# Attention of the later pairs: 128-row chunks with whole scores and one running state, in place of 64-row blocks on quadrants of the array

## The chip, the cores and the metric

The kernel runs on one core of one Trainium2 chip. The metric is the device time of one execution in microseconds. A core has TensorE (PE; its weight loads are shown apart as PEld), VectorE (DVE), ScalarE (ACT), GpSimd (POOL) and SyncE (SP), which run side by side and wait for each other by semaphores. SyncE issues nearly all DMA transfers here.

## The reference, cut to what matters

Retention without a softmax (8 batches, 8 heads, 576 positions, head size 64), and then a mixer of low rank over the positions with a two-layer network:

```
Dmat[h, i, j] = gamma[h] ** (i - j)  if i >= j else 0
x  = ((q @ k.T / 8) * Dmat) @ v                    # heads side by side: 8 x 576 x 512
u  = x + (x.T @ U @ V).T                           # U: 576 x 32, V: 32 x 576
out = u + relu(u @ w_ch1) @ w_ch2                  # 512 -> 2048 -> 512
```

Since gamma ** (i - j) is gamma ** i times gamma ** -j, the kernel scales v by gamma ** -j ahead and the result by gamma ** i behind. What remains of Dmat is a triangular mask, and what lies before a block enters as a state, the running sum of k.T @ v.

## The kernel before, in words

Batches are taken two at a time, as a pair of 2 x 576 = 9 x 128 rows: chunks 0 to 3 are of the even batch, 5 to 8 of the odd one, and chunk 4 (J) holds the last 64 rows of the one and the first 64 of the other. Pair 0 is computed by functions of its own in the start-up and the first stretch (lines 603 to 1009), which the change doesn't touch. Pairs 1 to 3, 27 chunks, go the way that is described here.

**A chunk's way.** `load` (229) fetches k, q and v, three DMAs on SyncE's queue. `prep` (586) casts them: k to bf16 on VectorE in three pieces, because one head of each pair of heads has its two half chunks exchanged between the partition halves (272), q on ScalarE (273), v times its scale on GpSimd in three pieces (281). Then `xbar` (288) transposes q and k with one DMA from SyncE's queue into qkT.

**Attention in sections.** `section(pr, i, n)` (396) works on two chunks at once: scores and states of chunk n, output of chunk i = n - 1. All its matmuls are 64x64 blocks on the four quadrants of TensorE, 64 in a full section: `SC` (305) the two diagonal blocks of the scores of each head, `ST` (367) the sums k.T @ v into AB, one for each half of a chunk, `RV` (325) masked scores times v, `QS` (337) query times state. Scores and output share one PSUM tile, pp, of which there is one. VectorE follows: `mask` (313), the states of the two halves as sums of AB and of an fp32 copy, Af, which ScalarE makes (385 to 394), xt (353), which frees pp for the next section, and two copies of queries to the other half of the partitions (347).

**The mixer.** `MA` (440) forms x.T @ U, `MH` (467) brings it back to the positions, VectorE adds x and gives u (473), and a transposing DMA on SyncE's queue turns u into uT (484), which the next batch's network reads. The odd batch has two such steps, of three and of two chunks.

**The network.** Y1 (523) multiplies uT by w_ch1 and ScalarE applies relu (528); Y2 (557) multiplies by w_ch2, VectorE adds u (546), and GpSimd's queue stores (549).

**What sets the order.** Nothing is scheduled for itself: instructions stand on each engine in the order in which Python issues them, and every queue is worked through in order. `merge` (16) interleaves. Its main list is the network of batch b, with nominal costs: an item of Y1 is 864 or 1080 ns, one of Y2 864, the list 27.6 us for an even batch and 34.6 us for an odd one. The fill list, attention and mixer of batch b + 1, is spread evenly over the first 0.82 of that cost: nine items before the change. The aux list, loads and preps two chunks ahead of a load, is spread over 0.64. The first such stretch has lists and leads of its own (1022 to 1031).

Of the kernel before, what the change touches and what calls it, by code (L numbers as in the profile page):

```python
# [9 lines left out]
FP32 = mybir.dt.float32  # L10
BF16 = mybir.dt.bfloat16
AF = mybir.ActivationFunctionType
# [24 lines left out]
def kernel(  # L37
# [11 lines left out]
    nc = tc.nc  # L49
# [18 lines left out]
    def pool(name, bufs, **kw):  # L68
        return ctx.enter_context(tc.tile_pool(name=name, bufs=bufs, **kw))
# [8 lines left out]
    q2_pool = pool("q2_pool", 2)  # L78
# [15 lines left out]
    triH = consts.tile([P, HALF], BF16, name="triH")  # L94
    Af = consts.tile([P, 2, NHP * D], FP32, name="Af")
# [21 lines left out]
    def early_consts():  # L117
# [32 lines left out]
        nc.vector.tensor_copy(out=triH[0:HALF], in_=tri[0:HALF, 0:HALF])  # L150
        nc.vector.tensor_copy(out=triH[HALF:P], in_=tri[HALF:P, HALF:P])
# [102 lines left out]
    def prep_v(pr, i, rows=slice(0, P)):  # L254
        c = ch[pr, i]
        if "v" not in c:
            c["v"] = v_pool.tile([P, H, D], BF16, tag="v", name="vt")
        scale_rows(c["v"][rows], c["f", 2], i, rows, nc.gpsimd)

    def moves():
        lo, hi = slice(0, HALF), slice(HALF, P)
        return ((slice(0, P), slice(0, P), 0), (lo, hi, 1), (hi, lo, 1))

    def cast_chunk(pr, i):
        c = ch[pr, i]
        c["qk"] = qk_pool.tile([P, 2, dm], BF16, tag="qk", name="qk")
        o = c["qk"][:, 1, :].rearrange("p (hp hl d) -> p hl hp d", hl=2, d=D)
        f = c["f", 1].rearrange("p (hp hl) d -> p hl hp d", hl=2)  # L270
        for to, fr, hl in moves():
            nc.vector.tensor_copy(out=o[to, hl], in_=f[fr, hl])  # L272
        nc.scalar.activation(  # L273
            out=c["qk"][:, 0, :], in_=c["f", 0].rearrange("p h d -> p (h d)"), func=AF.Copy)
        c["v"] = v_pool.tile([P, H, D], BF16, tag="v", name="vt")
        o = c["v"].rearrange("p (hp hl) d -> p hl hp d", hl=2)
        f = c["f", 2].rearrange("p (hp hl) d -> p hl hp d", hl=2)
        w = vscale[:, i, :].rearrange("p (hp hl) -> p hl hp", hl=2)
        for to, fr, hl in moves():
            n = fr.stop - fr.start  # L280
            nc.gpsimd.tensor_tensor(  # L281
                out=o[to, hl], in0=f[fr, hl],
                in1=w[fr, hl, :, None].to_broadcast([n, NHP, D]), op=ALU.mult)

# [9 lines left out]

    def half(n):
        return slice(n * HALF, (n + 1) * HALF)

    def SC(c, pp):  # L300
        qkT = c["qkT"]
        for hp in range(NHP):
            for hl in range(2):
                for m in range(2):
                    nc.tensor.matmul(  # L305
                        pp[half(m), m ^ hl, hp * D:(hp + 1) * D],
                        qkT[half(hl), NHP + hp, half(m)], qkT[half(hl), hp, half(m ^ hl)],
                        start=True, stop=True,
                    )

    def mask(c, pp):
        ret = ret_pool.tile([P, 2, NHP, D], BF16, tag="ret", name="ret")
        nc.vector.tensor_tensor(  # L313
            out=ret.rearrange("p a b i -> p a (b i)").rearrange(
                "p a (b i) -> p a b i", i=D),
            in0=pp[:, :, 0:NHP * D].rearrange("p a (b i) -> p a b i", i=D),
            in1=triH[:, None, None, :].to_broadcast([P, 2, NHP, D]), op=ALU.mult,
        )
        c["ret"] = ret

    def RV(c, pp):
        for hp in range(NHP):
            for hl in range(2):
                for m in range(2):
                    nc.tensor.matmul(  # L325
                        pp[half(m ^ hl), hl, NHP * D + hp * D:NHP * D + (hp + 1) * D],
                        c["ret"][half(m), m ^ hl, hp, :], c["v"][half(m), 2 * hp + hl, :],
                        start=(hp == 0), stop=True, skip_group_check=True,
                    )

    def QS(c, pp, ts):
        for hp in range(NHP):
            for hl in range(2):
                for t in ts:
                    r = half(hl ^ t)
                    qt = c["q2"][r, hp, :] if t else c["qkT"][r, hp, half(t)]
                    nc.tensor.matmul(  # L337
                        pp[half(t), hl, NHP * D + hp * D:NHP * D + (hp + 1) * D],
                        qt, c["S"][r, t, hp, :],
                        start=False, stop=True, skip_group_check=True,  # L340
                    )

    def queries(c):

        c["q2"] = q2_pool.tile([P, NHP, D], BF16, tag="q2", name="q2")
        for x in range(2):
            nc.vector.tensor_copy(  # L347
                out=c["q2"][half(x)], in_=c["qkT"][half(1 - x), 0:NHP, half(1)])

    def XS(pr, i, pp):  # L350
        if ("x", pr) not in st:
            st["x", pr] = x_pool.tile([P, NI, dm], BF16, tag="x", name="xt")
        nc.vector.tensor_tensor(  # L353
            out=st["x", pr][:, i, :].rearrange("p (hp hl d) -> p hl hp d", hl=2, d=D),
            in0=pp[:, :, NHP * D:2 * NHP * D].rearrange("p hl (hp d) -> p hl hp d", d=D),
            in1=qscale[:, i, :].rearrange("p (hp hl) -> p hl hp", hl=2)[
                :, :, :, None].to_broadcast([P, 2, NHP, D]),
            op=ALU.mult,
        )

    def ST(steps):

        for hp in range(NHP):
            for hl in range(2):
                for c, t, start in steps:
                    m, h = t ^ hl, 2 * hp + hl
                    nc.tensor.matmul(  # L367
                        st["AB"][half(hl), t, hp * D:(hp + 1) * D],
                        c["qk"][half(m), 1, h * D:(h + 1) * D], c["v"][half(m), h, :],
                        start=(start and hp == 0), stop=True, skip_group_check=True,  # L370
                    )

    def states(c, i):


        A, Bk = st["AB"][:, 0, 0:NHP * D], st["AB"][:, 1, 0:NHP * D]
        now, old = i % 2, 1 - i % 2
        c["S"] = s_pool.tile([P, 2, NHP, D], BF16, tag="s_sb", name="s_sb")
        S_ = c["S"].rearrange("p s hp d -> p s (hp d)")
        if i == 0:  # L380
            for x in range(2):
                nc.scalar.activation(
                    out=S_[half(x), 1, :], in_=A[half(1 - x)], func=AF.Copy)
        if i != J:
            nc.scalar.activation(out=Af[:, now, :], in_=A, func=AF.Copy)  # L385
        if i == J + 1:
            nc.scalar.activation(out=S_[:, 0, :], in_=Bk, func=AF.Copy)  # L387
        elif i != 0:
            nc.vector.tensor_tensor(out=S_[:, 0, :], in0=Bk, in1=Af[:, old, :], op=ALU.add)
        if i not in (0, J):  # L390
            for x in range(2):
                nc.vector.tensor_tensor(  # L392
                    out=S_[half(x), 1, :], in0=Bk[half(1 - x)],
                    in1=Af[half(1 - x), now, :], op=ALU.add)

    def section(pr, i, n):

        pp = ps_sc.tile([P, 2, 2 * NHP * D], FP32, tag="psc", name="pp")
        if n is not None:
            c = ch[pr, n]  # L400
            SC(c, pp)
            steps = []
            if n in (0, J + 1):
                st["AB"] = ps_o.tile([P, 2, 2 * NHP * D], FP32, tag="po", name="AB")
            if n != J:
                steps.append((c, 0, n in (0, J + 1)))
            if n != 0:
                steps.append((ch[pr, n - 1], 1, n in (1, J + 1)))
            ST(steps)
        if i is not None:  # L410
            RV(ch[pr, i], pp)
            QS(ch[pr, i], pp, {0: (1,), J: (0,)}.get(i, (0, 1)))
        if n is not None:
            mask(c, pp)
            states(c, n)
        if i is not None:
            XS(pr, i, pp)
        if n is not None and n != J:
            queries(c)

    def attn_items(pr, par):
        ks = list(range(0, J + 1) if par == 0 else range(J + 1, NI))
        return [
            lambda i=i, n=n: section(pr, i, n) for i, n in zip([None] + ks, ks + [None])]
# [161 lines left out]
    def prep(g):  # L586
        pr, i = order[g]
        cast_chunk(pr, i)
        xbar(pr, i)
# [421 lines left out]
    with tc.manual_schedule():  # L1011
# [7 lines left out]
        def ready(n):  # L1019
# [10 lines left out]
            starts=(0.3, 0.05, 0.92), leads=(0.81, 0.56, 1.0),  # L1030
# [42 lines left out]
```

## Time and profile before

| | us |
|---|---|
| time, median of 3 runs | 351.9 (349.24 to 354.42) |
| time of the profiled execution | 351.9 |
| its span in the profile | 349.7 |
| TensorE busy | 319.7 (91%) |
| VectorE busy | 174.0 (50%) |
| ScalarE busy | 137.3 (39%) |
| GpSimd busy | 101.5 (29%) |
| mean granted TensorE clock | 0.985 |

Costs per instruction (mean ns of one), of the operations that the change touches:

| line, engine, operation | ns |
|---|---|
| L313 DVE mask, 128x512 | 691 |
| L689 DVE mask of pair 0, 128x1024 | 1222 |
| L389, L392 DVE states, 128x256 and 64x256 | 414, 422 |
| L353 DVE xt, 128x512 | 690 |
| L347 DVE query copies, 64x256 | 261 |
| L272 DVE casts of k, 128x256 and 64x256 | 360, 324 |
| L244 DVE cast of 64x512 | 397 |
| L385 ACT copy of a state sum, 128x256 | 383 |
| L938 ACT copy out of PSUM, 128x512 | 595 |
| L281 POOL scaled v, 128x256 and 64x256 | 623, 612 |
| L248 POOL scaled v, 64x512 | 1041 |
| L473 DVE u, 128x1024, 128x768, 128x512 | 1217, 953, 686 |

A row of the profile's groups names the source line, the engine, what is written from what, and the shape. A wait names who waited, for whom, the sum in us, how often and the longest. Time in a wait costs only where the waiting engine is the bound. Matmuls of TensorE overlap, so their durations don't add; the distance from the start of one group to the start of the next is what a group costs.

### The profile page before, as it was taken

How to read it: one execution, taken by the hardware profiler on the slowest of the kernel's cores; microseconds unless marked ns; L12 is line 12 of the kernel's file. 1: busy time of each engine (PE TensorE's matmuls, PEld its weight loads, DVE VectorE, ACT ScalarE, POOL GpSimd, SP SyncE). 2: the span in 40 equal slices, each digit the busy share in tenths (PEclk: the TensorE clock that was granted, in tenths of full speed). 3: DMA queues.
4: the chain of work that ended last, by engine and by line, in shares of the span. 5: the costliest groups of instructions: out<-in, count | busy, mean ns of one | idle time of the engine just before them, and what ended most of it. 6: DMA issues, size and time to landing. Idle time of an engine off the chain costs nothing.

```text
span 349.7 us, 9092 instructions
## 1 busy us (share of the span) xinstructions
PE 319.7 (91%) x3870; PEld 172.7 (49%) x3870; DVE 174.0 (50%) x358; ACT 137.3 (39%) x298; POOL 101.5 (29%) x169
## 2 busy tenths in 40 slices
PE   8989799999999779979699986988979998999996
PEld 3564445754444334447454443436744454457644
DVE  7654256329743877337554396623955276510021
ACT  3547447871010653047520354107741075017500
POOL 7676760422113622141221314023225120010000
PEclk9999899999999999989989999999999999999999
DMA  7999999984956896937989368996599801240012
GB/s 224 225 212 238 209 206 201 194 154 96 264 150 159 178 210 133 228 80 144 169 160 237 108 125 119 178 221 144 116 174 249 175 32 35 64 128 5 0 62 90
DMA packets 152376, 53.30 MB, mean 152 GB/s; under 512 B 132016, under 2 KB 149808, under 8 KB 152336
## 3 DMA queue, kind: packets, MB, share of 16 engines
q1 hardware_dynamic: 144512, 40.40, 61.1%
q0 software_dynamic: 7824, 12.32, 14.5%
q8 instruction: 30, 0.49, 0.6%
q14 instruction: 10, 0.08, 0.1%
HBM read 36.85 MB, written 9.44 MB: 132 GB/s over the span
## 4 chain that ended last, share of the span: by engine, by line
PE 65%; DMA 19%; DVE 6%; SPq 3%; issue 2%; POOL 2%; ACT 1%; POOLq 0%; DVEq 0%
PE ps_y L557 31%; PE ps_y L523 26%; DMA qkT<-qk 10%; DMA uT<-u 4%; DMA stage_t<-in_q_dram 3%; SPq L617 2%; DMA U_f<-in_moe_U_dram 2%; PE pp L305 2%; DVE s_sb L392 2%; DVE xt L353 1%; PE pp L337 1%; PE ps_y L568 1%; PE ph L467 1%; SPq L229 1%; PE pp L325 1%
## 5 line engine op out<-in xcount | busy, mean ns | idle before, releaser
L528 ACT ACTIVATE y<-ps_y 128x384 bf16<-128x384 f32 (+2 forms) x192 | 90.5, 490 | 135.7 <-PE ps_y L523 135.0
L523 PE MATMUL ps_y<-uT,w_sb 128*128 128x256 bf16 (+2 forms) x768 | 137.4, 333 | 4.8 <-DMA uT<-u 4.6
L557 PE MATMUL ps_y<-w_sb,y 128*128 128x512 bf16 x560 | 126.0, 379 | 0.0
L523 PEld LDWEIGHTS <-w_sb 128*128 128x128 bf16 x768 | 73.0, 99 | 53.7 <-DMA uT<-u 5.6
L557 PEld LDWEIGHTS <-y 128*128 128x128 bf16 x560 | 52.9, 98 | 61.7
L281 POOL TENSOR_TENSOR vt<-stage_t,vscale 64x256 bf16<-64x256 f32 (+1 forms) x81 | 49.9, 616 | 83.2 <-DMA stage_t<-in_v_dram 78.7
L546 DVE TENSOR_TENSOR o_sb<-ps_y,u 128x512 f32<-128x512 f32 (+2 forms) x38 | 25.2, 662 | 81.8 <-PE ps_y L557 79.6
L549 POOL DMA_DIRECT2D out_dram<-o_sb x31 | 17.4, 560 | 114.9 <-DVE o_sb L546 106.0
L313 DVE TENSOR_TENSOR ret<-pp,triH 128x512 bf16<-128x512 f32 x27 | 18.7, 691 | 41.9 <-PE pp L305 21.9
L473 DVE TENSOR_TENSOR u<-ph,xt 128x768 bf16<-128x768 f32 (+2 forms) x24 | 21.8, 952 | 16.8 <-PE ph L467 16.8
L272 DVE CAST qk<-stage_t 64x256 bf16<-64x256 f32 (+1 forms) x81 | 27.2, 336 | 2.6 <-DMA stage_t<-in_k_dram 1.4
L305 PE MATMUL pp<-qkT 64*64 64x64 bf16 x432 | 8.8, 201 | 15.1 <-DMA qkT<-qk 13.8
L353 DVE TENSOR_TENSOR xt<-pp,qscale 128x512 bf16<-128x512 f32 x27 | 18.6, 690 | 4.1 <-PE pp L337 3.6
L305 PEld LDWEIGHTS <-qkT 64*64 64x64 bf16 x432 | 5.9, 110 | 25.5 <-DMA qkT<-qk 18.3
L392 DVE TENSOR_TENSOR s_sb<-AB,Af 64x256 bf16<-64x256 f32 x42 | 17.7, 422 | 1.2 <-ACT s_sb L387 0.7
L273 ACT ACTIVATE qk<-stage_t 128x512 bf16<-128x512 f32 x27 | 16.7, 624 | 2.2 <-DMA stage_t<-in_q_dram 2.2
L385 ACT ACTIVATE Af<-AB 128x256 f32<-128x256 f32 x24 | 9.2, 383 | 16.7 <-PE AB L367 15.8
L689 DVE TENSOR_TENSOR ret<-psc,triU 128x1024 bf16<-128x1024 f32 x8 | 9.6, 1222 | 12.2 <-PE psc L681 12.2
L347 DVE COPY q<-qkT 64x256 bf16<-64x256 bf16 x48 | 12.5, 261 | 1.1
L635 POOL CAST qk<-stage_t 128x512 bf16<-128x512 f32 x16 | 9.7, 616 | 6.4 <-DMA stage_t<-in_v_dram 3.5
L193 PE MATMUL pw<-ident 128*128 128x512 bf16 x31 | 9.8, 461 | 1.4 <-POOL ident masks.py:199 1.4
L446 ACT ACTIVATE a_sb<-pa 128x128 bf16<-128x128 f32 x8 | 2.2, 278 | 21.6 <-PE pa L440 21.6
(112 smaller groups left out, 202.2 us busy)
## 6 DMA issues: line engine op xcount, KB each, us to landing
stage_t<-in_k_dram SPq DMA_DIRECT2D x32, 256.0 KB, 4.7
stage_t<-in_q_dram SPq DMA_DIRECT2D x32, 256.0 KB, 4.8
stage_t<-in_v_dram SPq DMA_DIRECT2D x32, 256.0 KB, 5.7
out_dram<-o_sb POOLq DMA_DIRECT2D x31, 256.0 KB, 3.8
w_sb<-in_moe_w_ch_dram POOLq DMA_DIRECT2D x12, 256.0 KB, 10.1
stage_t<-in_k_dram SPq DMA_DIRECT2D x8, 128.0 KB, 3.4
stage_t<-in_q_dram SPq DMA_DIRECT2D x8, 128.0 KB, 3.4
stage_t<-in_v_dram SPq DMA_DIRECT2D x8, 128.0 KB, 3.4
```

What stands on the lines that cost most here:

```text
L272: nc.vector.tensor_copy(out=o[to, hl], in_=f[fr, hl])
L281: nc.gpsimd.tensor_tensor(out=o[to, hl], in0=f[fr, hl], in1=w[fr, hl, :, None].to_broadcast([n, NHP, D]), op=ALU.mult)
L305: nc.tensor.matmul(pp[half(m), m ^ hl, hp * D:(hp + 1) * D], qkT[half(hl), NHP + hp, half(m)], qkT[half(hl), hp, half(m ^ hl)], start=True ...
L313: nc.vector.tensor_tensor(out=ret.rearrange("p a b i -> p a (b i)").rearrange("p a (b i) -> p a b i", i=D), in0=pp[:, :, 0:NHP * D].rearra ...
L353: nc.vector.tensor_tensor(out=st["x", pr][:, i, :].rearrange("p (hp hl d) -> p hl hp d", hl=2, d=D), in0=pp[:, :, NHP * D:2 * NHP * D].rea ...
L392: nc.vector.tensor_tensor(out=S_[half(x), 1, :], in0=Bk[half(1 - x)], in1=Af[half(1 - x), now, :], op=ALU.add)
L473: nc.vector.tensor_tensor(out=st["u", par][:, i0 - base:i0 - base + n, w].rearrange("p s (c d) -> p c s d", c=2), in0=ph[k][:, :, 0:n, :], ...
L523: nc.tensor.matmul(ps[:, 0:n, :], w1_sb[:, cc, f * P:(f + 1) * P], st["uT", par][:, c0:c0 + n, cc, :], start=(cc == 0), stop=(cc == NCC - 1),)
L528: nc.scalar.activation(out=st["y1", par][:, f, c0 * P:(c0 + n) * P], in_=ps[:, 0:n, :].rearrange("p s t -> p (s t)"), func=AF.Relu)
L546: nc.vector.tensor_tensor(out=o_sb[:, 0:n], in0=ps[:, 0:n], in1=st["u", par][:, c, w], op=ALU.add)
L549: (nc.sync if last else nc.gpsimd).dma_start(out=out_flat[r0:r0 + P, w], in_=o_sb[:, 0:n])
L557: nc.tensor.matmul(ps, st["y1", par][:, f, c * P:(c + 1) * P], w2_sb[:, f, :], start=(f == 0), stop=(f == NF - 1),)
```

## The change

Sections go. A chunk has two items, A and B. A issues the scores of the whole 128x128 block of each head (eight matmuls, 64 rows of the array each), the query by state (eight) into a PSUM tile of its own, po, and the mask of 128x1024 elements. B issues masked scores times v (eight matmuls on the whole array, 64 columns), xt, the state sum of the whole chunk (four matmuls on the whole array), and a ScalarE copy of the running state to bf16. There is one state per batch, kept in PSUM, in place of two sums per chunk. Of chunk J, the mask is block diagonal (triJ), the query by state comes in B and on its first 64 rows alone, and the state sum of its last 64 rows is an item of its own, SJ. The mixed placement of half chunks goes, so k is cast and v is scaled in one instruction each (`cast_qk` and `prep_v`, which pair 0's chunk J uses already), and the copies of queries go. The fill list has 13 items in place of nine. In the first stretch with sections it starts at 0.2 of the cost in place of 0.3.

The diff, cut to its core:

```diff
-    q2_pool = pool("q2_pool", 2)
...
-    triH = consts.tile([P, HALF], BF16, name="triH")
-    Af = consts.tile([P, 2, NHP * D], FP32, name="Af")
+    triJ = consts.tile([P, P], BF16, name="triJ")
...
-        nc.vector.tensor_copy(out=triH[0:HALF], in_=tri[0:HALF, 0:HALF])
-        nc.vector.tensor_copy(out=triH[HALF:P], in_=tri[HALF:P, HALF:P])
+        nc.vector.tensor_copy(out=triJ, in_=tri)
+        nc.vector.memset(triJ[0:HALF, HALF:P], 0.0)
...
-    def moves():
...
-    def cast_chunk(pr, i):
...
-    def SC(c, pp):
+    def SC(pr, i):
+        c = ch[pr, i]
         qkT = c["qkT"]
+        psc = ps_sc.tile([P, 2, NHP, P], FP32, tag="psc", name="psc")
         for hp in range(NHP):
             for hl in range(2):
...
+                r = slice(hl * HALF, (hl + 1) * HALF)
+                nc.tensor.matmul(
+                    psc[:, hl, hp, :], qkT[r, NHP + hp, :], qkT[r, hp, :],
+                    start=True, stop=True,
+                )
+        c["psc"] = psc
...
+    def mask(pr, i):
+        c = ch[pr, i]
+        ret = ret_pool.tile([P, H, P], BF16, tag="ret", name="ret")
+        m = triJ if i == J else tri
         nc.vector.tensor_tensor(
...
+            out=ret.rearrange("p (hp hl) i -> p hl hp i", hl=2), in0=c["psc"],
+            in1=m[:, None, None, :].to_broadcast([P, 2, NHP, P]), op=ALU.mult,
         )
         c["ret"] = ret
...
+    def QS(pr, i):
+        c = ch[pr, i]
+        if "po" not in c:
+            c["po"] = ps_o.tile([P, 2, dm], FP32, tag="po", name="po")
+        s_sb = st["s_sb"]
+        m = slice(0, HALF) if i == J else slice(0, P)
         for hp in range(NHP):
             for hl in range(2):
...
+                r = slice(hl * HALF, (hl + 1) * HALF)
+                nc.tensor.matmul(
+                    c["po"][m, hl, hp * D:(hp + 1) * D],
+                    c["qkT"][r, hp, m], s_sb[r, hp, hl * D:(hl + 1) * D],
+                    start=(i != J and hp == 0), stop=True, skip_group_check=True,
+                )
+
+    def RV(pr, i):
...
+                h = 2 * hp + hl
+                nc.tensor.matmul(
+                    c["po"][:, hl, hp * D:(hp + 1) * D],
+                    c["ret"][:, h, :], c["v"][:, h, :],
+                    start=(first and hp == 0), stop=True, skip_group_check=True,
+                )
...
-    def queries(c):
...
+    def ST(pr, i):
...
+        rows = slice(HALF, P) if i == J else slice(0, P)
+        vf = c["v"].rearrange("p h d -> p (h d)")
         for hp in range(NHP):
...
+            nc.tensor.matmul(
+                st["S"][:, hp, :],
+                c["qk"][rows, 1, hp * P:(hp + 1) * P], vf[rows, hp * P:(hp + 1) * P],
+                start=(i in (0, J) and hp == 0), stop=True, skip_group_check=True,
+            )
+
+    def Scopy(pr, i):
+        s_sb = s_pool.tile([P, NHP, P], BF16, tag="s_sb", name="s_sb")
+        nc.scalar.activation(out=s_sb, in_=st["S"], func=AF.Copy)
+        st["s_sb"] = s_sb
...
-    def states(c, i):
...
-    def section(pr, i, n):
...
     def attn_items(pr, par):
...
+        items = []
+
+        def A(i):
+            SC(pr, i)
+            if i not in (0, J):
+                QS(pr, i)
+            mask(pr, i)
+
+        def Bf(i):
+            RV(pr, i)
+            if i == J:
+                QS(pr, i)
+            XS(pr, i)
+            if i not in (J, NI - 1):
+                ST(pr, i)
+                Scopy(pr, i)
+
+        def SJ():
+            ST(pr, J)
+            Scopy(pr, J)
+
+        if par == 1:
+            items.append(SJ)
+        for i in (range(0, J + 1) if par == 0 else range(J + 1, NI)):
+            items.append(lambda i=i: A(i))
+            items.append(lambda i=i: Bf(i))
+        return items
...
     def prep(g):
         pr, i = order[g]
-        cast_chunk(pr, i)
+        cast_qk(pr, i)
+        prep_v(pr, i)
         xbar(pr, i)
...
-            starts=(0.3, 0.05, 0.92), leads=(0.81, 0.56, 1.0),
+            starts=(0.2, 0.05, 0.92), leads=(0.81, 0.56, 1.0),
```

More of the change, by code (lines that the diff above doesn't have):

```diff
@@ L258, in prep_v @@
         scale_rows(c["v"][rows], c["f", 2], i, rows, nc.gpsimd)
-    def moves():
-        lo, hi = slice(0, HALF), slice(HALF, P)
-        return ((slice(0, P), slice(0, P), 0), (lo, hi, 1), (hi, lo, 1))
-    def cast_chunk(pr, i):
[L267 to L283, printed above, removed]
     def xbar(pr, i):
@@ L292 @@
     st = {}
-    def half(n):
-        return slice(n * HALF, (n + 1) * HALF)
-    def SC(c, pp):
+    def SC(pr, i):
+        c = ch[pr, i]
         qkT = c["qkT"]
+        psc = ps_sc.tile([P, 2, NHP, P], FP32, tag="psc", name="psc")
         for hp in range(NHP):
             for hl in range(2):
[L304 to L309, printed above, removed]
@@ L311, in mask @@
-    def mask(c, pp):
-        ret = ret_pool.tile([P, 2, NHP, D], BF16, tag="ret", name="ret")
+                r = slice(hl * HALF, (hl + 1) * HALF)
[8 more added lines that the diff above has]
+        m = triJ if i == J else tri
@@ L313, in mask @@
         nc.vector.tensor_tensor(
[L314 to L317, printed above, removed]
+            out=ret.rearrange("p (hp hl) i -> p hl hp i", hl=2), in0=c["psc"],
+            in1=m[:, None, None, :].to_broadcast([P, 2, NHP, P]), op=ALU.mult,
         )
         c["ret"] = ret
-    def RV(c, pp):
+    def QS(pr, i):
[4 more added lines that the diff above has]
+        m = slice(0, HALF) if i == J else slice(0, P)
@@ L322, in RV @@
         for hp in range(NHP):
             for hl in range(2):
[L324 to L331, printed above, removed]
+                r = slice(hl * HALF, (hl + 1) * HALF)
[4 more added lines that the diff above has]
+                )
@@ L332, in QS @@
+    def RV(pr, i):
+        c = ch[pr, i]
+        if "po" not in c:
+            c["po"] = ps_o.tile([P, 2, dm], FP32, tag="po", name="po")
+        first = i in (0, J)
         for hp in range(NHP):
             for hl in range(2):
[L334 to L341, printed above, removed]
@@ L343, in queries @@
-    def queries(c):
[L345 to L350, printed above, removed]
+                h = 2 * hp + hl
[4 more added lines that the diff above has]
+                )
@@ L351, in XS @@
+    def XS(pr, i):
+        c = ch[pr, i]
         if ("x", pr) not in st:
             st["x", pr] = x_pool.tile([P, NI, dm], BF16, tag="x", name="xt")
+        xt = st["x", pr]
         nc.vector.tensor_tensor(
-            out=st["x", pr][:, i, :].rearrange("p (hp hl d) -> p hl hp d", hl=2, d=D),
-            in0=pp[:, :, NHP * D:2 * NHP * D].rearrange("p hl (hp d) -> p hl hp d", d=D),
+            out=xt[:, i, :].rearrange("p (hp hl d) -> p hl hp d", hl=2, d=D),
+            in0=c["po"][:, :, 0:NHP * D].rearrange("p hl (hp d) -> p hl hp d", d=D),
@@ L359, in XS @@
         )
-    def ST(steps):
-        for hp in range(NHP):
[L364 to L371, printed above, removed]
-    def states(c, i):
[L376 to L394, printed above, removed]
@@ L396, in section @@
-    def section(pr, i, n):
[L398 to L419, printed above, removed]
@@ L421, in attn_items @@
-    def attn_items(pr, par):
-        ks = list(range(0, J + 1) if par == 0 else range(J + 1, NI))
-        return [
-            lambda i=i, n=n: section(pr, i, n) for i, n in zip([None] + ks, ks + [None])]
+    def ST(pr, i):
+        c = ch[pr, i]
+        if i in (0, J):
+            st["S"] = ps_s.tile([P, NHP, P], FP32, tag="pss", name="pss")
+        rows = slice(HALF, P) if i == J else slice(0, P)
+        vf = c["v"].rearrange("p h d -> p (h d)")
+        for hp in range(NHP):
+            nc.tensor.matmul(
[3 more added lines that the diff above has]
+            )
```

## The prediction

> **What bounds the kernel now.** I read the page's busy line and the chain first, then the waits of TensorE, then the timelines of VectorE, SyncE and TensorE in one stretch, then the granted clock.
>
> ```profile
> PE 319.7 (91%) x3870; PEld 172.7 (49%) x3870; DVE 174.0 (50%) x358; ACT 137.3 (39%) x298; POOL 101.5 (29%) x169
> PE 65%; DMA 19%; DVE 6%; SPq 3%; issue 2%; POOL 2%; ACT 1%; POOLq 0%; DVEq 0%
> ```
>
> TensorE is the bound: 319.7 of 349.7 us. The chain still gives a quarter to DMA and VectorE, so TensorE's idle time is worth placing. Its waits:
>
> ```profile
> PE pp L305 <- DMA qkT<-qk: 13.8, 8, 3.0
> PE ps_y L523 <- DMA uT<-u: 4.6, 2, 2.5
> PE pp L305 <- DVE xt L353: 1.1, 3, 0.7
> ```
>
> Summed over 5 us windows, TensorE is idle 6.6 us before 60 us (the start-up) and 20.5 us from 60 to 345 us: 15.9 us in the attention sections, 4.6 us at the hand-over uT. Why is qkT late? VectorE from 203 us:
>
> ```profile
> 203.54 0.69 DVE L313 TENSOR_TENSOR ret<-pp,triH 128x512 bf16<-128x512 f32 x1
> 204.15 0.41 DVE L389 TENSOR_TENSOR s_sb<-AB,Af 128x256 bf16<-128x256 f32 x1
> 204.58 0.86 DVE L392 TENSOR_TENSOR s_sb<-AB,Af 64x256 bf16<-64x256 f32 x2
> 205.47 0.69 DVE L353 TENSOR_TENSOR xt<-pp,qscale 128x512 bf16<-128x512 f32 x1
> 206.19 0.46 DVE L347 COPY q<-qkT 64x256 bf16<-64x256 bf16 x2
> 206.68 0.90 DVE L272 CAST qk<-stage_t 128x256 bf16<-128x256 f32 x3
> 207.61 0.69 DVE L313 TENSOR_TENSOR ret<-pp,triH 128x512 bf16<-128x512 f32 x1
> ```
>
> There is no gap: a section with a cast costs VectorE 4.07 us (203.54 to 207.61). TensorE would need 3.4 us (twelve Y1 matmuls 2.76 and the section 0.65). So VectorE falls behind, its cast of k ends late, and the transpose starts behind it. The chain's next lines:
>
> ```profile
> 207.64 5.01 DMA qkT<-qk
> 212.70 0.32 PE pp L305 x16
> ```
>
> The transpose goes out 0.06 us after that cast, and TensorE stands until it has landed. Now TensorE's price of a section:
>
> ```profile
> 158.82 0.32 PE L305 MATMUL pp<-qkT 64*64 64x64 bf16 x16
> 158.97 0.30 PE L367 MATMUL AB<-vt,qk 64*64 64x64 bf16 x16
> 159.10 0.30 PE L325 MATMUL pp<-vt,ret 64*64 64x64 bf16 x16
> 159.46 0.82 PE L523 MATMUL ps_y<-uT,w_sb 128*128 128x384 bf16 x4
> ```
>
> From first start to the next Y1, 64 small matmuls take 0.64 us. Last, the clock, in 2 us windows after the two longest stalls (second figure: TensorE busy; third from the end: the clock):
>
> ```profile
> 154.00:156.00 2.00, 2.00 (x30) 1.17 (x20) 1.67 (x5) 1.77 (x5) 0.71 (x2) 0.50 0.03 8
> 174.00:176.00 2.00, 1.95 (x60) 1.38 (x61) 0.83 (x2) 0.00 (x0) 1.18 (x2) 0.50 1.25 249
> ```
>
> TensorE is busy, but at half clock. Over 150 to 160 and 170 to 180 us the means are about 0.82 and 0.83: 10 x 0.18 + 10 x 0.17 = 3.5 us more that these stalls cost.
>
> [...] its half clock follows 2.2 and 3.0 us of idle time. [...] here 16 matmuls of L708 take 0.34 us where 32 take 0.57, so 16 cost 0.23 and the switch about 0.11.[...]
>
> **The change, part by part.** It touches only pairs 1 to 3, 27 chunks; start-up, first stretch and last stretch keep their instructions (the mask constants exchange two small VectorE copies for a copy and a memset, nothing on a path).
>
> *TensorE.* Before: per pair seven full sections of 0.65 and four end ones of about 0.36, 6.0 us, so 18.0 in all. After, with 0.12 us per switch of tile mode, columns at the rate of L708 (two row halves at once) and L717 (8 full 128-column matmuls in 0.55, less the switch 54 ns each):
> - scores: 8 of 64x128 by 128 columns, two at once: 4 x 54 ns + 0.12 = 0.34; x27 = 9.2.
> - query by state: 8 by 64 columns, two at once, 0.11 in the same mode; x21 = 2.3; the half chunk alone, 3 x 0.24 = 0.7.
> - ret by v: 8 full loads with only 64 columns each. No row shows this. From below 27 ns (L756, 64 rows, 8 in 0.34 with a switch), from above 69 ns (L717 with its switch left in), 98 if nothing of the load is hidden. I take 43, the stream plus 16: 0.34; x27 = 9.3 (5.8 to 14.9, 21).
> - states: 4 x 55 ns = 0.22; x24 = 5.3, and 0.4 for the half chunk's switches.
>
> Sum 27.2: **TensorE gains 9.2 us of work** (5.7 to 15).
>
> *VectorE.* Per chunk before: mask 0.69, states 0.41 + 2 x 0.42, xt 0.69, query copies 2 x 0.26, casts 0.36 + 2 x 0.32: 4.2 us. After: a mask of 1024 elements 1.22 (row L689), xt 0.69, one cast, no row of this shape, 0.40 (the 64x512 one) to 0.7 with both halves of today's: 2.3 to 2.6. The state becomes one ScalarE copy of 0.60 in place of 0.38, nothing on a path. GpSimd scales v in one instruction of about 1.04 instead of 1.85.
>
> *Order.* Nine fill items per stretch become thirteen on the same lead (0.82 of 27.6 or 34.6 us of nominal work), so two main items now lie between scores and ret by v. Chunks are 3.5 or 4.4 us apart, not 2.5 or 3.1, while casts and transposes keep their places. In the stretch from 112 us the last chunk's cast stands at 6.0 nominal us; its scores move from 9.5 to 13.8. The least slack from cast to scores becomes 6.9 us plus about 1.5 of attention work. What has to fit is about 1 of cast and queue, 1 of issue and 3.8 (median) to 5 of landing. So the 15.9 us go. What I keep is 1.5 us for the new wait, ret by v for its mask: behind it stand the states and all later Y1 on TensorE, and the state copy on ScalarE. The mask needs 1.22 and about 0.1 on each side; two Y1 tiles take 1.84 us, and no cast stands between scores and mask. The next scores need the mask only, and the next query by state needs the xt and state copy, two items earlier. Net **-14.4**.
>
> *SyncE and uT.* The mixer's last fill moves from 0.683 to 0.725 of the stretch, 1.2 to 1.5 us nearer to the end. But today the second uT transpose stands behind three loads on SyncE's queue (142.35 to 145.41); after, those loads are issued ahead of the first uT transpose. Counting on from the second mixer step: sums of u about 2.1, issue 0.6 later behind the first transpose (2.6 us each), landing 5.8 to 6.4, so 8.5 to 9.1 us against 8.1 of cover: 0.4 to 1.0 us in two stretches, 0.2 to 0.5 where u has four chunks, 3.0 in all instead of 4.6. **-1.6**, from +2 to -4.
>
> *Clock.* With no stall over 2 us the two half-clock spells go: **-3.4**, or nothing if a long stall stays.
>
> Sum on the profiled execution: 349.7 + 9.2 - 14.4 - 1.6 - 3.4 = 339.5 of span. Its time is 351.9, 2.2 above its span and equal to the median: **341.7, say 341.5**.
>
> **Rivals.** *The mask as a new bound (slower).* If VectorE starts a mask late, TensorE waits at ret by v, 27 times. The cover leaves about 0.4 us. Over 2% slower is 359, 17.5 us above my sum: 0.65 us per chunk, so masks that start 1.05 us late. With 1.2 us late it is 27 x 0.8 = 21.6: 363 us. For it: VectorE is in order, and a cast that waits for its load holds up everything; the DMA share is over 1 in several windows. Against: VectorE's casts wait for loads only 1.4 us today, and its load falls by 40%. 0.17. *Weight loads bind (no change).* Ret by v at 69 and states at 69 ns add 5.6 + 1.3: 348.5; at 98 ns, 11.9 + 4.1: 357.5. Against: rows L717 and L734 hide most of the load. 0.16. *Transposes stay late (no change).* If half the 15.9 us and the slow clock stay: 341.5 + 8 + 3.4 = 353. For it: the DMA engines hold the loads, and a transpose took 7.3 us at worst; against: the slack. 0.12. That the change does not do what it says: its words on start-up have no counterpart in the diff; the attention part does.
>
> **How the numbers follow.** Measurement can tell about 2% (344.9 and 358.9). Mine has 0.55, own range 336 to 345, and is all of "faster"; the two rivals of no change have 0.28; the mask has 0.17. The range goes from 334 (ret by v at 27 ns, uT at its best: 341.5 - 3.5 - 2.4 = 335.6, and a little more clock) to 357, which leaves the mask and a few hundredths out.
>
> **What would show it.** Right: waits of scores for qkT under 2 us; VectorE near 125 us busy; TensorE busy for the new matmuls about 1 us per chunk against 0.65; no half clock after 60 us; ret by v waiting for its mask under 0.1 us each. Wrong: "PE po <- DVE ret" of ten us or more, spacing of ret by v near 70 or 100 ns, or uT stalls above 2 us each.

## The result, and the profile after

The changed kernel takes 330.2 us (median of 4 runs, 329.95 to 333.76), the kernel before 353.2 beside it (median of 4): ratio 0.941, interval 0.929 to 0.953. One of these four runs of before (354.6) fell in a slower state of the chip, and all ratios and intervals here compare the means of the fast runs alone, so that they are not quotients of the medians. The profiled execution takes 330.4 us with a span of 328.3. The direction was forecast; the size was not: 341.5 us with a lower end of 334.

The busy line, the slices of the clock and the chain, from the page of after:

```profile
PE 318.1 (97%) x2958; PEld 176.3 (54%) x2958; DVE 135.4 (41%) x193; ACT 138.9 (42%) x289; POOL 79.8 (24%) x115
...
PEclk9999999999999999999999999999999999999999
...
PE 86%; DMA 6%; SPq 3%; POOL 2%; issue 1%; DVE 1%; ACT 1%; DVEq 0%
```

TensorE is busy for 1.6 us less than before (318.1 against 319.7) although the span lost 21.4: time went out of its gaps. The DMA share of the chain went from 19% to 6%, and no slice has a lower clock. All waits of TensorE, of after:

```profile
PE pst L604 <- POOL qk L589: 1.8, 2, 1.6
PE pw L191 <- POOL ident masks.py:199: 1.4, 1, 1.4
PE pst L710 <- POOL qk L242: 1.0, 1, 1.0
PE pst L604 <- POOL qk L593: 0.9, 2, 0.7
PE pss L688 <- ACT sblk L698: 0.5, 1, 0.5
PE pa L393 <- DVE xt L679: 0.5, 1, 0.5
PE xT L884 <- ACT a_sb L399: 0.4, 1, 0.4
PE psc L635 <- DVE qkT L616: 0.3, 1, 0.3
PE ps_y L476 <- ACT uT L451: 0.2, 1, 0.2
```

Every one belongs to the start-up or the first stretch. Neither scores for qkT, nor ret by v for its mask, nor Y1 for a transposed uT is among them: in the 5 us windows from 60 to 325 us TensorE is busy all of the time (the last row is uT made by ScalarE at 54 us). TensorE in a stretch of after, answering to the section shown in the prediction (L274 scores, L299 query by state, L313 ret by v, L339 states):

```profile
187.38 0.40 PE L274 MATMUL psc<-qkT 64*128 64x128 bf16 x8
187.62 0.28 PE L299 MATMUL po<-s_sb,qkT 64*128 64x64 bf16 x8
187.83 1.90 PE L476 MATMUL ps_y<-uT,w_sb 128*128 128x512 bf16 x8
189.57 0.40 PE L313 MATMUL po<-vt,ret 128*128 128x64 bf16 x8
189.80 0.39 PE L339 MATMUL pss<-vt,qk 128*128 128x128 bf16 x4
190.02 1.89 PE L476 MATMUL ps_y<-uT,w_sb 128*128 128x512 bf16 x8
```

From start to start, A costs 0.45 us, B 0.45 us, of which ret by v is 0.23. VectorE in the same place:

```profile
187.82 1.23 DVE L284 TENSOR_TENSOR ret<-psc,tri 128x1024 bf16<-128x1024 f32 x1 [3.19 <-PE psc L274]
190.00 0.69 DVE L324 TENSOR_TENSOR xt<-po,qscale 128x512 bf16<-128x512 f32 x1 [0.95 <-PE po L313]
190.61 0.42 DVE L242 CAST qk<-stage_t 128x512 bf16<-128x512 f32 x1
192.28 1.22 DVE L284 TENSOR_TENSOR ret<-psc,tri 128x1024 bf16<-128x1024 f32 x1 [1.26 <-PE psc L274]
```

A chunk now takes 2.3 us of VectorE in a period of 4.46, and each of its instructions but the cast has waited for TensorE: VectorE is ahead, where before it had no gap. The mask ends at 189.05, ret by v starts at 189.57.

### The profile page after: what moved, and what is told of

It is laid out like the page before. It is cut to its first block, busy times and chain, and to the rows that moved or that the text cites. A ratio compares the mean times of both kernels' runs of the same rounds, so it can differ in the third digit from the quotient of the medians.

```text
span 328.3 us, 7041 instructions
## 1 busy us (share of the span) xinstructions
PE 318.1 (97%) x2958; PEld 176.3 (54%) x2958; DVE 135.4 (41%) x193; ACT 138.9 (42%) x289; POOL 79.8 (24%) x115
## 4 chain that ended last, share of the span: by engine, by line
PE 86%; DMA 6%; SPq 3%; POOL 2%; issue 1%; DVE 1%; ACT 1%; DVEq 0%
PE ps_y L510 38%; PE ps_y L476 37%; DMA stage_t<-in_q_dram 4%; PE psc L274 3%; DMA U_f<-in_moe_U_dram 3%; SPq L571 2%; PE po L313 2%; PE pss L339 2%; PE ph L420 1%; PE ps_y L521 1%; SPq L227 1%; PE po L299 1%; PE pa L393 1%; ACT uT L451 0%; DVE xt L679 0%
## 5 line engine op out<-in xcount | busy, mean ns | idle before, releaser
L284 DVE TENSOR_TENSOR ret<-psc,tri 128x1024 bf16<-128x1024 f32 x24 | 29.4, 1225 | 53.2 <-PE psc L274 53.2
L246 POOL TENSOR_TENSOR vt<-stage_t,vscale 128x512 bf16<-128x512 f32 (+1 forms) x29 | 30.4, 1056 | 79.3 <-DMA stage_t<-in_v_dram 60.0
L426 DVE TENSOR_TENSOR u<-ph,xt 128x768 bf16<-128x768 f32 (+2 forms) x24 | 21.8, 951 | 15.9 <-PE ph L420 15.9
L324 DVE TENSOR_TENSOR xt<-po,qscale 128x512 bf16<-128x512 f32 x27 | 18.6, 690 | 22.2 <-PE po L313 21.3
L347 ACT ACTIVATE s_sb<-pss 128x512 bf16<-128x512 f32 x24 | 14.3, 596 | 12.8 <-PE pss L339 11.7
L240 ACT ACTIVATE qk<-stage_t 128x512 bf16<-128x512 f32 (+1 forms) x28 | 17.3, 622 | 2.4 <-DMA stage_t<-in_q_dram 2.4
L242 DVE CAST qk<-stage_t 128x512 bf16<-128x512 f32 (+1 forms) x28 | 13.9, 502 | 0.0
L313 PEld LDWEIGHTS <-ret 128*128 128x128 bf16 x216 | 10.0, 98 | 4.5 <-DVE ret L284 0.2
L274 PEld LDWEIGHTS <-qkT 64*128 64x128 bf16 x216 | 6.1, 94 | 9.5 <-issue 8.9
L274 PE MATMUL psc<-qkT 64*128 64x128 bf16 x216 | 10.7, 219 | 0.0
L313 PE MATMUL po<-vt,ret 128*128 128x64 bf16 x216 | 10.7, 193 | 0.0
```

The source lines that it names most:

```text
L240: nc.scalar.activation(out=o, in_=f, func=AF.Copy)
L246: eng.tensor_tensor(out=o, in0=f[rows], in1=vscale[rows, i, :, None].to_broadcast([n, H, D]), op=ALU.mult)
L274: nc.tensor.matmul(psc[:, hl, hp, :], qkT[r, NHP + hp, :], qkT[r, hp, :], start=True, stop=True,)
L284: nc.vector.tensor_tensor(out=ret.rearrange("p (hp hl) i -> p hl hp i", hl=2), in0=c["psc"], in1=m[:, None, None, :].to_broadcast([P, 2, N ...
L313: nc.tensor.matmul(c["po"][:, hl, hp * D:(hp + 1) * D], c["ret"][:, h, :], c["v"][:, h, :], start=(first and hp == 0), stop=True, skip_gro ...
L324: nc.vector.tensor_tensor(out=xt[:, i, :].rearrange("p (hp hl d) -> p hl hp d", hl=2, d=D), in0=c["po"][:, :, 0:NHP * D].rearrange("p hl ( ...
```

## The experiments

Two theories. **Order**: the stalls of before came from where the sections stood, too close to each other for VectorE and too soon behind the casts; the thirteen slots (places of the fill list) removed them. **Rate**: they came from VectorE's 4.2 us per section, and the lighter VectorE removed them. The first four kernels ran beside each other and before (350.7 us there).

**Places alone, instructions of before (b_spread).**

```diff
-        return [
-            lambda i=i, n=n: section(pr, i, n) for i, n in zip([None] + ks, ks + [None])]
+        items = [lambda: None] * len(ks * 2) + [lambda: None] * par
+        for j, (i, n) in enumerate(zip([None] + ks, ks + [None])):
+            at = min(2 * j + par, len(items) - 1)
+            items[at] = lambda i=i, n=n: section(pr, i, n)
+        return items
...
-            starts=(0.3, 0.05, 0.92), leads=(0.81, 0.56, 1.0),
+            starts=(0.2, 0.05, 0.92), leads=(0.81, 0.56, 1.0),
```

> The sections of the kernel before, unchanged in their instructions, but with empty fill items between them, so that scores, the mixer and both uT transposes stand at the places that they have after the change (and the first merged stretch starts at 0.2). Order theory: the stalls came from sections 2.5 us apart, closer than VectorE's 4.07 us and too soon behind the casts; spread out, the waits of scores for qkT fall from 13.8 to under 2 us, the uT waits from 4.6 to under 1, no half clock, and since 64 quadrant matmuls are cheaper than the new ones by some 5 us the time is 326 to 332 us. Rate theory: 4.2 us of VectorE work per chunk is itself the cause; the qkT and VectorE waits stay above 8 us, and the time is 338 to 346 us.

Measured: 331.8 us, 0.949 (0.944 to 0.955). TensorE's waits in it, the rows that bear on attention and uT:

```profile
PE pp L325 <- DVE xt L353: 2.9, 3, 1.0
PE ps_y L526 <- DMA uT<-u: 2.1, 2, 1.4
...
PE pp L337 <- DVE q L347: 0.8, 1, 0.8
...
PE pp L305 <- DMA qkT<-qk: 0.4, 1, 0.4
```

qkT went from 13.8 to 0.4 us with not one attention instruction changed. The order theory holds; the rate theory, as a needed cause, falls. Of what is left idle (9.7 us from 60 us on) 5.0 us are xt and uT: the last section stood only one slot behind its predecessor, with VectorE still at 4.2 us each. Some 1.8 us are gaps of 0.16 us where the trace lacks a matmul (3844 of 3870 have a record), and so are not idle time.

**VectorE's load put back (a_load).**

```diff
+    pad = consts.tile([P, 704], FP32, name="pad")
...
+    def extra():
+        nc.vector.tensor_tensor(
+            out=pad, in0=pad, in1=pad, op=ALU.add)
...
             mask(pr, i)
+            extra()
...
             XS(pr, i)
+            extra()
```

> The kernel after, with two VectorE additions of 704 fp32 elements per chunk on a scratch tile, one behind the mask (ahead of the cast) and one behind xt: about 1.8 us more, so VectorE has 4.1 us per chunk again, as before. Order theory: the places are wide enough (chunks 4.5 us apart on TensorE), so TensorE waits under 2 us in all and the time stays at 330 to 333 us. Rate theory: stalls of 8 us or more come back, and the time is 338 to 345 us.

Measured: 330.8 us, 0.946 (0.941 to 0.951), as the changed kernel. Its busy line, where VectorE is above the 174.0 us of before:

```profile
PE 317.0 (96%) x2935; PEld 176.6 (54%) x2958; DVE 178.6 (54%) x248; ACT 138.8 (42%) x289; POOL 80.2 (24%) x115
```

Some 40 us of VectorE work saved bought nothing by themselves at these places.

**VectorE relieved, order of before (b_relief).**

```diff
         for to, fr, hl in moves():
-            nc.vector.tensor_copy(out=o[to, hl], in_=f[fr, hl])
+            e = nc.vector if hl == 0 else nc.gpsimd
+            e.tensor_copy(out=o[to, hl], in_=f[fr, hl])
...
-            nc.vector.tensor_copy(
-                out=c["q2"][half(x)], in_=c["qkT"][half(1 - x), 0:NHP, half(1)])
+            nc.scalar.activation(
+                out=c["q2"][half(x)], in_=c["qkT"][half(1 - x), 0:NHP, half(1)],
+                func=AF.Copy)
```

> The kernel before with its order kept, but VectorE relieved: both query copies go to ScalarE, and the two half pieces of the cast of k to GpSimd. VectorE then has about 3.0 us per section with a cast in place of 4.2, under TensorE's 3.4. Rate theory: the attention stalls fall from 15.9 to under 5 us and the slow clock with one of its two spells; 335 to 343 us. Order theory: the slack from cast to scores (3.5 to 5 us of nominal work) is too short for a transpose of 4 to 5 us even when the cast is on time; 10 us or more of the stalls stay; 346 to 353 us.

Measured: 340.7 us, 0.975 (0.969 to 0.981). The time lies in the span of the rate theory, but the wait lies nearer to the other, and the profile still has two spells of half clock (117 to 120 and 206 to 209 us; mean clock 0.73 in 115 to 120 and 0.66 in 205 to 210):

```profile
PE pp L306 <- DMA qkT<-qk: 8.8, 7, 2.7
PE ps_y L525 <- ACT y L530: 2.6, 3, 1.4
```

With VectorE at 140.7 us, 8.8 of 13.8 us of the qkT wait stay. The rate was a part of the lateness; that the rest is order, this run alone doesn't show, because the work that was moved comes late on its new engines. Ahead of one of the stalls (2.2 us, up to 204.57) the chain of b_relief goes through ScalarE, where the cast of q (L274), which the transpose needs as well, stands behind two query copies (L348):

```profile
196.74 0.41 ACT q L348
...
198.69 0.53 ACT qk L274
...
199.27 5.26 DMA qkT<-qk
```

**Places of before, instructions of after (a_tight)**: the last leads, 0.82 to 0.57. The first stretch with sections stays wide; the eight qkT stalls of before all lie behind it, from 119 us on.

```diff
-                leads=(0.82, 0.64 if b < 6 else 0.3))
+                leads=(0.57, 0.64 if b < 6 else 0.3))
```

> The kernel after with the fill spread over 0.57 in place of 0.82 of the main list, so that chunks come about as close as sections did before and only about one main item stands between scores and ret by v. Price of the mask by the prediction: cover of one tile (0.92 or 1.15 us) against 1.22 + 0.2, so 0.3 to 0.5 us on each of the 22 chunks of these stretches, 7 to 11 us of waits for the mask. Rate theory: VectorE is light, so qkT waits stay under 3 us; 337 to 343 us. Order theory: qkT waits of 8 us or more come on top; 345 to 355 us.

Measured: 339.2 us, 0.972 (0.965 to 0.978), 9 us above the changed kernel.

```profile
PE psc L274 <- DMA qkT<-qk: 4.3, 5, 2.3
...
PE po L313 <- DVE ret L284: 1.4, 6, 0.2
```

```profile
114.19 0.41 PE L313 MATMUL po<-vt,ret 128*128 128x64 bf16 x8 [0.24 <-DVE ret L284]
```

The stalls come back with a light VectorE, and with ScalarE and GpSimd lighter than in b_relief. The time lies in the span of the rate theory, but not by its parts: the qkT wait is between what the two theories said, and the mask cost 1.4 us in place of 7 to 11. It is 0.24 us where one tile lay between (at 114.19, after A had ended at 112.91: the mask's answer takes 1.28 us from there, near the 1.31 that follows from the prediction's 1.22 + 0.2 less the query by state), and nothing where several chunks still had two tiles or a wider one between.

Taken together: at the places of before, a lighter VectorE gains 2.5% (b_relief) or 2.8% (a_tight, with the new matmuls paid for). At the wide places the kernel gains 5.1 to 5.4% with the heavy VectorE already (b_spread, a_load), and a light one adds little: 330.2 us against 331.8, and these two did not run beside each other. Wide places are enough alone; a light VectorE alone gets about half of it.

**uT nearer to the hand-over (a_late)**: the same line with 0.92.

> The changed kernel with the fill spread over 0.92 in place of 0.82 of the main list, so that the last mixer step and uT come 2.5 us (even stretches) or 3.1 us (odd ones) nearer to the hand-over. With the cover as the prediction counted it (8.5 to 9.1 us needed behind the second mixer step, 9.6 behind the single one), TensorE waits about 3 us for uT in each of five hand-overs, with slow clock behind some: 15 us or more, 344 to 350 us. If the transposes land sooner when no loads are in flight (4.2 to 4.8 us, issue 1.3 to 2.4), what is needed is 6.5 to 7.5 us: 1 to 2 us per hand-over, 335 to 340 us.

Measured: 332.5 us, 0.956 (0.950 to 0.962); the changed kernel beside it (a_again) 330.1. Both numbers that I had were too high. SyncE's only row from 133 to 146 us, and TensorE over the same hand-over:

```profile
137.03 3.35 SPq L437 DMA_TRANSPOSE uT<-u  x2
```

```profile
137.51 0.29 PE L420 MATMUL ph<-a_sb,V 32*128 32x128 bf16 x8
137.73 4.49 PE L510 MATMUL ps_y<-w_sb,y 128*128 128x512 bf16 x19
142.06 2.34 PE L476 MATMUL ps_y<-uT,w_sb 128*128 128x384 bf16 x16
```

From the second mixer step to Y1 there are 4.55 us, and Y1 doesn't wait, nor do its narrower tiles 0.7 us later. What is needed is under 5.3 us, not 8.5 to 9.1: the sums of u end 1.6 us after the step, both transposes have left the queue 3.35 us after the first began, and SyncE issues no load from 133 to 146 us. The median from issue to landing of uT is 5.8 us before, 4.8 after and 3.9 here. That the loads make the difference fits these places, but no run changes the loads alone, and at the last hand-over of after, where SyncE issues none (279 to 292 us), it is still 4.2 us. Only two hand-overs of four chunks waited, about 1.1 us each (for one of them the profile names a cast of VectorE, but uT was issued at 179.03, 4.8 us before Y1 went on at 183.85, and its landings in this run take 3.1 to 5.1 us).

**Can sections beat the change?** A full section is cheaper on TensorE (0.65 against 0.9 us), so a spread version without its xt and uT waits should be the fastest. Five attempts; the changed kernel ran once more beside the first two (a_again 330.1) and beside the next two (a_third 330.6).

> The changed kernel once more, beside the others: 330 us, no idle time of TensorE between 60 us and the end, and the first Y1 stretch of 92 matmuls starting near 57 us (in the profile of before a slow clock at 40 to 44 us had put this start-up off by 2 us, which is chance and not the change).

> The changed kernel beside the two evenly spread ones on the same chip: 330 us.

b_spread_relief joins b_spread and b_relief; b_spread_q takes of the latter only the query copies.

> The sections of before at the places of the change, and VectorE relieved too (query copies on ScalarE, two of the three pieces of the cast of k on GpSimd). Theory that order and rate are two halves of one lateness: what is left idle when only spread (some 7 us: late xt, late uT) goes too, and TensorE's work is about 5 us less than after the change, so 325 to 328 us, under the changed kernel. Rival, that the work of the quadrant matmuls is no less in time than it looks, or that GpSimd's casts come late behind its stores: 330 us or more.

> As the spread kernel with sections, with the query copies alone moved to ScalarE (0.52 us of VectorE's 4.2 per section). If the lateness left is VectorE's few tenths per section, this is enough: xt waits under 1 us, 326 to 329 us. If GpSimd's share of the casts is needed: 330 to 332 us.

Measured: 332.3 and 332.3 us, 0.956 (0.949 to 0.963) and 0.957 (0.949 to 0.965), above what I expected of both. TensorE's first two waits in b_spread_q say why:

```profile
PE ps_y L527 <- ACT y L532: 4.1, 6, 1.4
PE pp L325 <- DVE xt L354: 2.9, 3, 1.0
```

The query copies on ScalarE hold up the relu that frees Y1's tiles, and xt after the last section is as late as it was.

b_even puts two slots behind every section; b_even_k also gives GpSimd part of the cast; b_last_k then moves the odd batches' sections one slot later.

```diff
...
+        items = [lambda: None] * (2 * len(ks) + 1)
+        for j, (i, n) in enumerate(zip([None] + ks, ks + [None])):
+            items[2 * j] = lambda i=i, n=n: section(pr, i, n)
...
# b_last_k: (2 * len(ks) + 1 + par) and items[2 * j + par]
```

> Sections of before, evenly spread: two fill slots from each section to the next, the last one too (in the first spread kernel it stood one slot behind its predecessor and TensorE waited about 1 us for xt, six times). Instructions as in before. Theory that the 5 us of cheaper TensorE work are real and were hidden by the xt and uT waits: those waits fall under 3 us, 326 to 329 us, under the changed kernel. Rival, that something else of the sections costs as much: 330 us or more.

> The evenly spread sections with two of the three pieces of the cast of k on GpSimd and the query copies left on VectorE (on ScalarE they had held up the relu of the odd stretches, 4.1 us). If VectorE's lateness still costs uT or xt: 1 to 2 us less than evenly spread alone; if not, the same within 1 us.

> As the evenly spread sections with part of the cast of k on GpSimd, but those of the odd batches one slot later, where scores stood in the first spread kernel and after the change. In the evenly spread kernels they stood one slot (1.7 us) earlier and the waits for qkT came back, 0.4 to 6.1 us. If that slot is the cause, qkT waits fall under 1 us again, xt waits stay under 1 us, and what is left is uT, 2 to 4 us: 327 to 330 us. If the sections carry another cost: 331 us or more.

Measured: 335.1, 332.5 and 334.4 us; 0.959 (0.953 to 0.965), 0.949 (0.943 to 0.956), 0.955 (0.951 to 0.960). b_even_k is 2.6 us under b_even, where I had said 1 to 2, with intervals that overlap. The xt waits went, and qkT came back. Two rows of TensorE's waits in b_even, then one in b_last_k:

```profile
PE pp L305 <- DMA qkT<-qk: 6.1, 5, 1.8
PE ps_y L525 <- DMA uT<-u: 4.2, 3, 1.7
```

```profile
PE pp L306 <- DMA qkT<-qk: 3.6, 3, 1.4
```

The places explain this better than I saw when I wrote the expectations. Of an odd batch, b_even and b_even_k put the first section into slot 0 where b_spread has it in slot 1. And where b_spread and the change have 13 slots in a stretch, b_last_k has 14 throughout and b_even has 14 for the even batches, so that a slot comes earlier there. So the sections stand nearer to the casts in all three, in b_last_k too. TensorE from the first Y1 matmul of a stretch to the first scores of an odd batch, in b_spread, b_even and b_last_k:

```profile
108.47 3.62 PE L526 MATMUL ps_y<-uT,w_sb 128*128 128x512 bf16 x16
109.28 1.89 PE L525 MATMUL ps_y<-uT,w_sb 128*128 128x512 bf16 x8
108.26 2.75 PE L526 MATMUL ps_y<-uT,w_sb 128*128 128x512 bf16 x12
```

After the change it is 16 as well. So b_last_k went back by one Y1 tile of four matmuls (0.9 us) and not by two, and in the next stretch the counts are 16, 8 and 8. The qkT waits, 0.4, 6.1 and 3.6 us, go in the order of these places, which speaks for order once more; how much of them the places make is open, since the profile of b_even is of its slowest run (338.4 us) and that of b_last_k of its fastest (331.7). A second cause may be at work: in b_last_k GpSimd's casts of k stand in its queue behind v of the chunk before (about 2 us), and so does the transpose behind them. That was not tried.

No version with sections has a median under the changed kernel's. Two come near: b_even_k has 332.5 us beside 330.6 (fastest runs 329.6 and 329.8), and b_spread 331.8, 0.5% above 330.2. Placing the sections of before anew gives all but about 2 us of what the change gives.

## Why the prediction was wrong, step by step

The bound, the cause and the direction were right: the 15.9 us of attention stalls and the two half-clock spells went, VectorE is at 135 us (about 125 was forecast), and the order of the thirteen slots is what did it, with VectorE's rate in second place. The range failed because four terms of the sum erred to one side:

| term | forecast us | measured us | off |
|---|---|---|---|
| TensorE's work | +9.2 | +4.7 | -4.5 |
| attention stalls left | 1.5 | 0 | -1.5 |
| uT stalls left | 3.0 | 0 | -3.0 |
| slow clock in the start-up of before | kept | gone | -2.1 |
| sum | | | -11.1 |

Forecast span 339.5, measured 328.3: 11.2 apart.

**Ret by v.** "I take 43, the stream plus 16." No row gave the 16; it was my estimate. It is 29 ns: eight in 0.23 us, 0.11 per chunk less, 27 x 0.11 = 3.0 of the 4.5. What I had set as the lower bound, 27 ns, was nearly the answer; it is an estimate too, eight of L756 in 0.34 us (15.03 to 15.37) less a switch. The other bound, 98 ns, is the duration of one load in before (L557, PEld). That a change of the tile mode costs 0.11 to 0.12 us was my estimate from L708: in before, 32 of its matmuls take 0.48 us up to a group of their own mode (17.47 to 17.95) and 0.57 us up to one of another (20.54 to 21.11). For the balance I take the time from the last transposes of the first stretch to the last Y2 part, both in the chain, before and then after:

```profile
57.76 0.45 PE pu L494 x8
343.24 3.55 PE ps_y L568 x48
```

```profile
55.62 0.45 PE pu L447 x8
321.87 3.55 PE ps_y L521 x48
```

Less idle time and clock that is 285.5 - 20.5 - 3.5 = 261.5 before, 266.2 after. The groups can also be summed one by one, from the first start to the next matmul of the network. The new ones take 24.4 us where I had 27.2; ret by v is all of that. The sections of before take 19.9 where I had 18.0: about 0.6 is their share of the half clock, and 1.1 lies in the last section of the odd batches, which takes 0.74 us and not 0.36 because TensorE pauses between its first two queries by state (131.54 to 131.88). The two ways agree to 0.4 us.

**The mask.** "What I keep is 1.5 us for the new wait." The arithmetic of the wait was right (a_tight), and so it should have been trusted: 0.5 us of margin per chunk and an idle VectorE leave nothing to keep. The rival that the mask becomes the bound finds nothing for it: VectorE stood idle for scores ahead of 26 of the 27 masks of after, and in a_load, with 43 us more work on it, TensorE's waits have no row for the mask.

**uT.** "Landing 5.8 to 6.4, so 8.5 to 9.1 us against 8.1 of cover." The landing was read from a stage in which three loads were under way, and I had seen that the change issues those loads ahead; I moved them in the queue and left the landing as it was. After, both transposes are one block on SyncE, the second goes out 2.0 us behind the step (135.59) in place of 2.7, they land in 5.3 and 4.6 us, and Y1 follows without a wait:

```profile
135.70 4.26 SPq L437 DMA_TRANSPOSE uT<-u  x2
```

```profile
135.95 7.08 PE L510 MATMUL ps_y<-w_sb,y 128*128 128x512 bf16 x32
142.87 2.34 PE L476 MATMUL ps_y<-uT,w_sb 128*128 128x384 bf16 x16
```

**The start-up.** I called it untouched and took its 2 us of slow clock with it. The profile of before has a clock of 0.65 and 0.50 in the windows 40:42 and 42:44 (third figure from the end):

```profile
42.00:44.00 2.00, 2.00 (x5) 0.46 (x3) 0.00 (x0) 0.67 (x2) 2.00 (x4) 0.50 0.89 153
```

That makes 1.7 of the 2.1 us. The profiles of the 13 other runs have 1.00 throughout the first 60 us, seven of them with the start-up instructions of before. I take it for chance of one execution, and a forecast on its own time carries it.

**The clock behind the stalls.** The 3.4 us went as forecast (no stall is left, and after has a clock of 1.00 in every 5 us window from 60 to 325 us), but my reading of what sets the half clock off was luck in part. The two spells did not follow the two longest stalls: 2.55 us of idle time up to 212.70 and 2.46 up to 237.05 are longer than the 2.15 ahead of the first spell, and full clock follows them.

```profile
212.00:214.00 2.00, 1.30 (x68) 0.91 (x69) 0.45 (x1) 0.38 (x1) 1.72 (x3) 1.00 1.29 230
```

In b_even half clock (128 to 131 us; mean clock 0.79 in 125 to 130 and 0.87 in 130 to 135) follows a stall of 1.8 us. So the length of one stall does not decide it in these runs, and "no stall over 2 us" was an estimate; what decides it is not shown.

The rival of binding weight loads is refuted (29 and 55 ns); that of late transposes was right in substance, since qkT does come back when scores stand one or two Y1 tiles nearer to the casts, but not at the places of this change.

## What to carry to other kernels

When an engine with 50% of the span holds up the bound, look at where its work stands before making it less: empty slots between the items took the qkT waits from 13.8 to 0.4 us with no instruction changed. A stall that is placed and measured should be taken off in full if the cover is worked out and holds, and a landing time is that of the place where it was measured: the median of uT was 5.8 us before and 4.8 after. A small gain on TensorE, such as the quadrant blocks' quarter microsecond per chunk, was lost again here by the waits that came with the sections. And a run that moves work from one engine to others also tests those others.

## What was not expected of the hardware

Eight matmuls with a full 128x128 load each and only 64 columns take 0.23 us, 29 ns each, though one load lasts 98 ns in its row:

```profile
L313 PEld LDWEIGHTS <-ret 128*128 128x128 bf16 x216 | 10.0, 98 | 4.5 <-DVE ret L284 0.2
```

And the transposing DMA of u lands in 3.9, 4.8 or 5.8 us (medians of three kernels) with the same bytes; what SyncE issues around it differs, but was not tried as the cause.
